# Both layers of the second MoE by one level of Strassen's scheme, with the sums of its weights' blocks parked in DRAM

## The chip, the cores and the metric

The kernel runs on one core of a Trainium2 chip. The metric is device time in microseconds (us) of one execution. Of the core's engines, TensorE (PE; its weight loads are listed as PEld) multiplies matrices, VectorE (DVE), ScalarE (ACT) and GpSimd (POOL) work on elements, and SyncE (SP) issues most DMAs.

## What is computed

Attention with a norm on q and k (4 batches, 12 heads, 448 positions, head size 64), then two MoE blocks one after the other on the 1792 x 768 result. The second is the one that changes:

```python
def _moe2_ref(x, w_in, w_out):      # x 1792x768, w_in 768x2048, w_out 2048x768
    h = x @ w_in
    relu6 = np.clip(h + 3.0, 0.0, 6.0)
    g = h * relu6 / 6.0
    return (g @ w_out).astype(np.float32)
```

Inputs and output are float32 on the host side, and the weights reach the chip as 64-bit floats, which the kernel decodes by integer operations on their two halves.

## The kernel before

Products that need float32's accuracy are made on float16: a matrix is scaled by a power of two and split into a high and a low part, and each product is three matmuls (high by high, low by high, high by low; `PROD`, L1208).

A planner (`Plan`) gets every step as an operation with its engine or engines, its dependencies, its buffer lease (`Ring`, `Lease`) and a modelled duration; it lists the steps by rank, shifted by offsets per stage (`CFG['off']`) and by a pace for the loads, and so writes one fixed order for each engine and for the DMA queue on SyncE. Where TensorE is expected to idle it adds filler matmuls on the identity (L1488).

The work goes by batch: attention, first MoE's input layer (L1218 in `in_block`, 448 columns), its output layer (L1271). Each batch's result (x2) is stored to DRAM. Attention of one batch is woven between the first MoE's matmuls of the one before. After the last batch the second MoE runs alone.

The second MoE goes over the tokens in five chunks (384 four times, then 256). Its input layer takes, for each of 16 blocks of 128 hidden features, 18 matmuls (6 blocks of 128 inputs by 3 parts) of the chunk's width into one PSUM bank (L1218); ScalarE's gate (L1364) reads the bank, VectorE multiplies (L1367), and the result is split into high (L410) and low (L425) in the tile gt. Its output layer takes, for each 128 tokens, 96 matmuls of 384 columns (L1385), copies the two banks out (L1404) and stores to the output (L1413).

The second MoE's weights W3 and W4 are prepared far ahead, within the batches from the first on (`Parked.add`, tile wc): 12 pieces of W3 are loaded as 128 x 1024 and 16 of W4 as 128 x 768 into two alternating buffers (wr), decoded by GpSimd (L525), VectorE (L532), ScalarE or GpSimd (L521, L516) and VectorE (L539), split with a common scale for each row, and stored as float16 parts (L649). When the first MoE's matmuls no longer need the SBUF places wa and wb, the parts are loaded back there (L681).

## Time and profile before

| what | us |
|---|---|
| median of 3 runs | 1240.18 (1237.2 to 1240.6) |
| span of the profiled execution | 1245.9 |
| TensorE busy | 1145.1 (92%) |
| VectorE busy | 757.2 (61%) |
| ScalarE busy | 705.1 (57%) |
| GpSimd busy | 393.6 (32%) |
| second MoE, first matmul to last | 801.4 to 1240.2 |

The profiled execution's span lies 5.7 us above the median of the runs. The profile is one execution; its views are the slices of the span, groups of instructions by source line and shape, busy time in windows, DMA issues, and the chain of work that ended last, followed back from the last instruction. A matmul's mean duration holds part of its neighbours', since matmuls overlap, so its share of time is the group's busy time over the count. TensorE's clock was at its upper level (2.4 GHz, granted share 1.00) in nearly all windows.

### The profile page before, as it was taken

Reading aid. Unit: us, or ns where it says so; the run is one execution under the profiler, and the core shown is the slowest. Engines: PE = TensorE matmul, PEld = TensorE weight load, DVE = VectorE, ACT = ScalarE, POOL = GpSimd, SP = SyncE. Lnnn points to the kernel's source line nnn. Section 1 sums busy time; section 2 is a strip of 40 time slices with the busy share of each in tenths; the row PEclk is TensorE's granted clock in tenths of the full one; section 3 lists DMA queues with packets and bytes.
Section 4 is the critical chain, followed back from the end, with each engine's and each line's share of the span. In section 5 each row is a group of like instructions: output and inputs, shape, how many; then the busy total and the mean of one; then the engine's idle time right before and its main releaser. Section 6 shows DMA issues by size and latency. Waiting matters only on the chain.

```text
span 1245.9 us, 19206 instructions
## 1 busy us (share of the span) xinstructions
PE 1145.1 (92%) x7151; PEld 654.0 (52%) x7151; DVE 757.2 (61%) x1326; ACT 705.1 (57%) x1512; POOL 393.6 (32%) x340
## 2 busy tenths in 40 slices
PE   2888898889797999989998899999999999999998
PEld 0555544444353455435454455566666666666684
DVE  7998799989889977699768775451041041041040
ACT  3888767888857787557778665541141141141140
POOL 6656667674747323456311221200000000000000
PEclk9999799999999999989999999999999999999999
DMA  6775567799986799866799876470100100100101
GB/s 177 209 192 175 175 193 205 170 193 221 224 261 185 186 193 229 262 188 191 155 193 247 240 252 225 137 215 14 47 18 13 46 19 14 40 12 13 26 1 26
DMA packets 253182, 180.05 MB, mean 145 GB/s; under 512 B 195488, under 2 KB 240544, under 8 KB 250016
## 3 DMA queue, kind: packets, MB, share of 16 engines
q1 hardware_dynamic: 251904, 177.66, 54.7%
q10 hardware_dynamic: 1184, 1.16, 0.4%
q8 instruction: 56, 0.92, 0.3%
q14 instruction: 38, 0.31, 0.1%
HBM read 96.01 MB, written 37.36 MB: 107 GB/s over the span
## 4 chain that ended last, share of the span: by engine, by line
PE 56%; DVE 8%; DMA 4%; issue 3%; ACT 2%; POOL 2%; SPq 1%; ACTq 0%; DVEq 0%; POOLq 0%
PE mm L1218 23%; PE s L1385 18%; PE mm L1271 10%; DMA arena<-phl 2%; PE mm L972 2%; DVE phl L425 1%; PE s L1011 1%; PE s L1014 1%; DVE smalls L782 1%; DMA arena<-in_q_dram 1%; POOL phl L440 1%; DVE arena L836 1%; DVE gt L425 1%; DVE st L1252 1%; ACT p L1024 1%
## 5 line engine op out<-in xcount | busy, mean ns | idle before, releaser
L1218 PEld LDWEIGHTS <-wa 128*128 128x128 f16 x2592 | 255.4, 99 | 193.4 <-issue 15.7
L1271 PE MATMUL mm<-gt,wb 128*128 128x448 f16 x1152 | 231.8, 356 | 10.1 <-POOL wb L440 4.0
L1218 PE MATMUL mm<-xt,wa 128*128 128x448 f16 x1152 | 231.0, 359 | 8.3 <-DVE st L1252 5.4
L1218 PE MATMUL mm<-arena,wa 128*128 128x384 f16 (+1 forms) x1440 | 219.6, 315 | 0.0
L1385 PE MATMUL s<-wb,gt 128*128 128x384 f16 x1344 | 219.2, 326 | 0.0
L1367 DVE SCALAR_TENSOR_TENSOR st<-st,mm 128x384 f32<-128x384 f32 (+1 forms) x80 | 42.1, 527 | 250.3 <-ACT st L1364 250.3
L1385 PEld LDWEIGHTS <-gt 128*128 128x128 f16 x1344 | 131.5, 98 | 86.8
L1271 PEld LDWEIGHTS <-wb 128*128 128x128 f16 x1152 | 112.6, 99 | 119.2 <-issue 6.1
L425 DVE SCALAR_TENSOR_TENSOR gt<-st,smalls,gt 128x448 f16<-128x448 f32 (+2 forms) x144 | 102.5, 717 | 51.7 <-ACT gt L410 50.5
L1024 ACT ACTIVATE p<-s,smalls 128x448 f32<-128x448 f32 x168 | 120.9, 721 | 17.6 <-DVE phl L425 6.6
L1404 ACT ACTIVATE p<-s,smalls 128x384 f32<-128x384 f32 x28 | 14.7, 577 | 199.6 <-PE s L1385 126.8
L410 ACT ACTIVATE gt<-st,smalls 128x384 f16<-128x384 f32 (+2 forms) x132 | 81.5, 621 | 78.3 <-DVE st L1367 46.0
L1019 DVE TENSOR_REDUCE smalls<-s 128x2 f32<-128x896 f32 (+1 forms) x96 | 92.0, 964 | 20.2 <-PE s L1014 19.7
L416 POOL TENSOR_SCALAR arena<-p,smalls 128x384 f16<-128x384 f32 (+1 forms) x13 | 9.9, 761 | 280.5 <-DMA p<-x2d 192.1
L1011 PE MATMUL s<-qkt 128*128 128x448 f16 (+1 forms) x192 | 62.9, 371 | 34.5 <-ACT p L1024 27.5
L1364 ACT ACTIVATE st<-mm,smalls 128x384 f32<-128x384 f32 (+1 forms) x80 | 51.7, 648 | 65.8 <-PE mm L1218 62.9
L425 DVE SCALAR_TENSOR_TENSOR phl<-p,smalls,phl 128x448 f16<-128x448 f32 x90 | 76.4, 875 | 9.6 <-ACT phl L410 5.7
L525 POOL TENSOR_SCALAR wc<-wr 128x1024 f32<-128x1024 f32 (+1 forms) x40 | 45.1, 1128 | 103.2 <-DMA wr<-in_moe_w_out_dram 75.2
L532 DVE SCALAR_TENSOR_TENSOR wc<-wr,wc 128x1024 uint32<-128x1024 uint32 (+1 forms) x40 | 46.9, 1171 | 31.7 <-POOL wc L525 31.7
L1014 PE MATMUL s<-qkt 128*128 128x448 f16 (+1 forms) x192 | 62.4, 366 | 0.0
L440 POOL TENSOR_TENSOR phl<-p,phl 128x448 f16<-128x448 f32 x31 | 43.4, 1409 | 49.4 <-ACT phl L410 43.4
L1073 PE MATMUL mm<-vhl,p 128*128 128x128 f32 x336 | 48.2, 299 | 9.5 <-ACT arena L1083 4.0
(165 smaller groups left out, 1566.1 us busy)
## 6 DMA issues: line engine op xcount, KB each, us to landing
wr<-in_moe_w_in_dram SPq DMA_DIRECT2D x16, 768.0 KB, 4.9
wr<-in_moe_w_out_dram SPq DMA_DIRECT2D x12, 1024.0 KB, 6.2
wr<-in_moe_w_in_dram SPq DMA_DIRECT2D x12, 1024.0 KB, 6.7
wr<-in_moe_w_out_dram SPq DMA_DIRECT2D x16, 768.0 KB, 4.7
qkd<-arena SPq DMA_DIRECT2D x18, 672.0 KB, 3.9
park_in<-wr SPq DMA_DIRECT2D x12, 512.0 KB, 4.4
park_out<-wr SPq DMA_DIRECT2D x16, 384.0 KB, 3.3
wa<-park_in SPq DMA_DIRECT2D x4, 1536.0 KB, 8.9
```

The costliest lines, as they stand in the source:

```text
L410: nc.scalar.activation(out=dst(), in_=src(), func=AF.Copy, scale=s)
L425: nc.vector.scalar_tensor_tensor(out=dst(), in0=src(), scalar=s, in1=high(), op0=ALU.mult, op1=ALU.subtract)
L440: (POOL, t_pool2(n), lambda: nc.gpsimd.tensor_tensor(out=lo(), in0=src(), in1=hi(), op=ALU.subtract)),
L1011: nc.tensor.matmul(o, lhsT=x[:, 64 * t:64 * t + m], rhs=x[:, 448:896], start=True, stop=False)
L1014: nc.tensor.matmul(o, lhsT=x[:, 64 * t:64 * t + m], rhs=x[:, 896:1344], start=False, stop=True)
L1019: nc.vector.tensor_reduce(out=nb, in_=s_t[sl.slot][:, :m, :S], axis=AX.X, op=ALU.max)
L1024: nc.scalar.activation(out=p(i), in_=s_t[sl.slot][:, i, :S], func=AF.Exp, bias=nb[:, i:i + 1], scale=alpha, accum_out=z[:, i:i + 1],)
L1073: nc.tensor.matmul(mm_t[tl.slot][:, 128 * j:128 * j + 128], lhsT=p(i)[:, c:c + 128], rhs=diag(), start=True, stop=True,)
L1218: nc.tensor.matmul(mm_t[ml.slot][:, :n], lhsT=w.inw(we, kc, f), rhs=x[:, xe, kc, :n], start=(kc == 0 and i == 0), stop=(kc == KD - 1 and i ...
L1271: nc.tensor.matmul(mm_t[ml.slot][:, :S], lhsT=W2.outw(we, fc, d * 128, 128), rhs=gv[:, ge_, fc, :], start=(fc == g.part.start and i == 0), ...
L1364: nc.scalar.activation(out=t, in_=m, func=AF.Relu, scale=ch.c3, bias=three)
L1385: nc.tensor.matmul(s_t[sl.slot][:, h, :half], lhsT=g[:, ge_, fc, tb * 128:tb * 128 + 128], rhs=W4.outw(we, fc, h * half, half), start=(fc ...
```

## The change

One level of Strassen's scheme (in Winograd's form) cuts each operand into 2 x 2 blocks, makes 7 products of sums of the blocks in place of 8 products of blocks, and gets the four blocks of the result by additions. Both layers of the second MoE are done so. The inner dimensions are halved: 768 into 2 x 384, the hidden 2048 first into two parts h (0 and 1), which are computed one after another, each of four `Quad`s (256 hidden features: two blocks of 128 by two halves of the chunk's tokens), and a `Pair` is 128 + 128 tokens by 2 x 384 outputs. There are three chunks of 768, 512 and 512 tokens. The turns are h = 0 for chunks 0, 1, 2, then h = 1 for chunks 2, 1, 0. The output sums of h = 0 are stored to a DRAM tile (part, L1785), loaded again with h = 1 (L1685) and added (L1735).

- A Quad has 7 products of 9 matmuls, each of half a chunk's columns (384 or 256), L1569; a Pair 7 of 12 with 384 columns, L1703. Bank 1 takes p1, p6, p5 and p3 on top of each other, and ScalarE copies it out between them (`keep`, L1589); the other results are additions on VectorE (L1582) into scratch, the gate (L1637) and product (L1640) run there, and seven sums (combine, L655) are split into high (L446, L452) and low (L669).
- The weights W3 and W4 come as 8 units each (128 x 1536 64-bit floats), one after another through one buffer: load L691, sign L703, decode L709, L719, L723, squares L739, four sums L655, high and low for 7 forms, store of 1344 KB L770. They begin after batch 1 (`wfrom`), not within batch 0, in the order W3 0 to 3, W4 0 to 3, W3 4 to 7, W4 4 to 7. The halves return by L778.
- x of a chunk is loaded (L1505, L1511), summed to 7 forms, split and stored once (L1529) for the second turn (L1537).
- Several tiles of SBUF are merged into larger ones, cut differently in different stages; the planner's numbers (`CFG`) are others. In the new order there are 131 filler matmuls instead of 202 (L1975).

```diff
-    CHUNKS = (384, 384, 384, 384, 256)
+    CHUNKS = (768, 512, 512)
+    FORMS = 7
+    HALF = 4
...
-    class Parked(Weight):
+    unit_ring, unit_loads, unit_stores = Ring(1), [], []
+    raw_u, set_u = cut(wr_m, 0, [128, 4 * LINE], I64), cut(wr_m, 12288, [128, 8, LINE], F32)
+    stage_u = cut(wr_m, 0, [128, 2, FORMS, LINE], F16)
...
+    class Combined:
...
+        def add(self, i, after):
+            n, here, unit = self.n, slice(i, i + 1), Lease(unit_ring)
...
+            o = sp(128 * n * (8 if self.wide else 4), load, after + unit_stores[-1:], takes=unit)
...
+            made = combine(self.left, lambda k: set_u[:, k], LINE, ends)
+            lows = []
+            for a, b in ((4, 7), (0, 4)):
+                flat = lambda t: t.rearrange("p a c -> p (a c)")
+                lows.append(parts(
...
+            self.stores[i] = sp(128 * 4 * FORMS * LINE, store, lows, gives=unit)
+            unit_stores.append(self.stores[i])
...
+    PAIRS = {1: (4, 4), 2: (5, 5), 3: (3, 6), 4: (6, 3), 5: (0, 0), 6: (1, 1), 7: (2, 2)}
+    BANK = {2: 0, 1: 1, 6: 1, 5: 1, 3: 1, 7: 2, 4: 2}
...
+    class Quad:
...
+            def emit():
+                for kc in range(3):
+                    for j, (we, xe) in enumerate(PROD):
+                        nc.tensor.matmul(
+                            self.bank(k), lhsT=w[:, we, fa, kc], rhs=self.ch.x[:, kc, xe, fb],
...
+        def keep(self, dst, deps, takes=None):
+            def emit():
+                nc.scalar.activation(out=self.held(dst), in_=self.bank(1), func=AF.Copy)
...
+        def p1(self):
+            self.product(1, [])
+            self.s1 = self.keep(0, [self.p[1]] + self.free, self.hold)
+        def p6(self):
+            self.product(6, [self.s1])
+            self.u2 = self.keep(1, [self.p[6], self.s1])
+        def p5(self):
+            self.product(5, [self.u2])
+            self.u4 = self.keep(2, [self.p[5], self.s1])
...
+        def p3(self):
+            self.product(3, [self.u4])
+            self.gate(7, 1, lambda: self.bank(1), [self.p[3]], self.banks[1])
...
+    def cycle(u, prev):
+        u.p1()
+        if prev is not None:
+            prev.p3()
+        u.p6()
+        if prev is not None:
+            prev.p4()
+        u.p5()
+        u.p7()
+        if isinstance(u, Pair):
+            u.p22()
+        u.p2()
...
-        if b == 0:
+        if b == CFG['wfrom']:
             off(7)
-            for i in range(W3.rows):
-                W3.add(i)
-            W3.add_scales(1.0)
+            for i in range(HALF):
+                W3.add(i, W2.done if i == 0 else [])
             off(8)
-            for i in range(W4.rows):
-                W4.add(i)
-            W4.add_scales(2.0 ** -21)
+            for i in range(HALF):
+                W4.add(i, [])
+            for i in range(HALF, 2 * HALF):
+                W3.add(i, [])
+            for i in range(HALF, 2 * HALF):
+                W4.add(i, [])
...
+    turns = [(0, ch) for ch in chunks] + [(1, ch) for ch in reversed(chunks)]
```

ScalarE in the second MoE. Before, in chunk 0 (st are float32 buffers, mm PSUM banks, gt the split result), gate and high part alternate:

```order
L1364 ACTIVATE st_72<-mm_92,smalls 128x384
L410 ACTIVATE gt<-st_72,smalls 128x384
L1364 ACTIVATE st_74<-mm_93,smalls 128x384
L410 ACTIVATE gt<-st_74,smalls 128x384
L1364 ACTIVATE st_73<-mm_90,smalls 128x384
```

Now, in a Quad of 256 columns (s_75 and s_76 are PSUM banks; p, st and wb hold scratch):

```order
L1589 ACTIVATE p<-s_75 128x256
L1637 ACTIVATE p<-st,smalls 128x768
L1589 ACTIVATE p<-s_75 128x256
L446 ACTIVATE gt<-p 128x768
L1589 ACTIVATE st<-s_76 128x256
L446 ACTIVATE gt<-p 128x1024
L1589 ACTIVATE st<-s_76 128x256
L1637 ACTIVATE wb<-s_75,smalls 128x256
```

The copies of bank 1 (L1589) now stand between gates and high parts of up to 1024 elements.

VectorE where the second MoE begins, before (product of the gate, low part):

```order
L1367 SCALAR_TENSOR_TENSOR st_72<-st_72,mm_92 128x384
L1367 SCALAR_TENSOR_TENSOR st_74<-st_74,mm_93 128x384
L405 TENSOR_SCALAR smalls<-smalls 128x1 x2
L425 SCALAR_TENSOR_TENSOR gt<-st_72,smalls,gt 128x384
L425 SCALAR_TENSOR_TENSOR gt<-st_74,smalls,gt 128x384
```

and now, in the first Quads of chunk 0:

```order
L1582 TENSOR_TENSOR p<-s_75,p 128x384
L1582 TENSOR_TENSOR p<-s_76,p 128x384
L709 SCALAR_TENSOR_TENSOR wr<-wr 128x768 x2
L1640 SCALAR_TENSOR_TENSOR wb<-wb,smalls,s_75 128x384
L723 SCALAR_TENSOR_TENSOR wr<-wr 128x768 x2
L1582 TENSOR_TENSOR p<-s_75,p 128x384
L655 TENSOR_TENSOR wr<-wr 128x384
```

Between the Quads' additions and gate products now stand decodes and sums of a unit of the weights (tile wr).

The DMA queue on SyncE near the end of the first MoE, before (park_out is W4's DRAM tile, x2d the first MoE's result):

```order
L649 DMA park_out<-wr_69 256x1x768
L1311 DMA x2d<-st_74 128x448
L509 DMA wr_69<-in_moe_w_out_dram 128x768
L1311 DMA x2d<-st_73 128x448
L649 DMA park_out<-wr_68 256x1x768
L649 DMA park_out<-wr_69 256x1x768
L681 DMA wb<-park_out 128x32x384 x2
```

and now:

```order
L770 DMA park_out<-wr 128x5376
L1529 DMA park_x_87<-xt 128x5376
L691 DMA wr<-in_moe_w_out_dram 128x1536
L1436 DMA x2d<-st 128x448
L778 DMA wb<-park_out 128x5376 x4
L770 DMA park_out<-wr 128x5376
L691 DMA wr<-in_moe_w_out_dram 128x1536
L770 DMA park_out<-wr 128x5376
```

Before, every piece of W4 was stored ahead of the reload into wb; now the last two units' stores stand behind it.

## Rows read from the trace of the kernel before

**Rows 1.** The page's slices of 31 us: busy tenths of two engines.
```profile
PE   2888898889797999989998899999999999999998
DVE  7998799989889977699768775451041041041040
```
**Rows 2.** The chain that ended last: start us, length us, what.
```profile
695.79 51.10 PE mm L1218 x270
746.89 54.48 PE mm L1271 x288
801.37 5.85 PE mm L1218 x36
...
1209.03 31.21 PE s L1385 x192
```
**Rows 3.** Groups of instructions by line and shape, TensorE: busy us, mean ns, idle before.
```profile
L1218 PE MATMUL mm<-arena,wa 128*128 128x384 f16 x1152 | 188.0, 326 | 0.0
L1218 PE MATMUL mm<-arena,wa 128*128 128x256 f16 x288 | 31.6, 273 | 0.0
L1385 PE MATMUL s<-wb,gt 128*128 128x384 f16 x1344 | 219.2, 326 | 0.0
L1218 PEld LDWEIGHTS <-wa 128*128 128x128 f16 x2592 | 255.4, 99 | 193.4 <-issue 15.7
L1488 PE MATMUL mm<-ident 128*128 128x512 bf16 x202 | 48.1, 388 | 1.2 <-DVE xt L1110 0.7 <-DVE smalls L390 0.5
```
**Rows 4.** Windows: us; busy us of PE, PEld, DVE, ACT, POOL; clock; DMA share; GB/s.
```profile
350.00:700.00 350.00, 322.42 (x2060) 167.90 (x2059) 287.08 (x504) 252.35 (x575) 139.93 (x121) 0.97 0.87 212
...
350.00:375.00 25.00, 25.00 (x135) 13.06 (x134) 23.07 (x43) 16.10 (x29) 13.61 (x12) 1.00 0.97 300
375.00:400.00 25.00, 20.45 (x101) 9.86 (x99) 24.27 (x48) 17.47 (x38) 17.31 (x13) 0.93 0.59 165
400.00:425.00 25.00, 20.57 (x101) 9.95 (x100) 24.15 (x35) 19.28 (x43) 11.72 (x11) 0.93 0.67 183
...
750.00:775.00 25.00, 25.00 (x134) 12.95 (x133) 11.13 (x23) 13.62 (x23) 4.94 (x5) 1.00 0.69 230
```
**Rows 5.** Groups by line and shape: ScalarE's and VectorE's steps on matrices.
```profile
L1364 ACT ACTIVATE st<-mm,smalls 128x256 f32<-128x256 f32 x16 | 9.0, 564 | 7.1 <-PE mm L1218 7.1
L410 ACT ACTIVATE wr<-wc,smalls 128x768 f16<-128x768 f32 x11 | 10.3, 933 | 4.1 <-DVE smalls L399 3.7
L410 ACT ACTIVATE wr<-wc,smalls 128x1024 f16<-128x1024 f32 x2 | 2.3, 1149 | 1.1 <-DVE smalls L399 1.1
L1367 DVE SCALAR_TENSOR_TENSOR st<-st,mm 128x256 f32<-128x256 f32 x16 | 6.7, 421 | 54.1 <-ACT st L1364 54.1
L425 DVE SCALAR_TENSOR_TENSOR gt<-st,smalls,gt 128x256 f16<-128x256 f32 x16 | 7.7, 484 | 9.2 <-ACT gt L410 9.2
L425 DVE SCALAR_TENSOR_TENSOR gt<-st,smalls,gt 128x384 f16<-128x384 f32 x64 | 39.7, 622 | 38.9 <-ACT gt L410 38.9
```
**Rows 6.** Groups by line and shape: decoding, low parts; last, GpSimd's in 350 to 700.
```profile
L532 DVE SCALAR_TENSOR_TENSOR wc<-wr,wc 128x768 uint32<-128x768 uint32 x16 | 15.3, 956 | 25.5 <-POOL wc L525 25.5
L425 DVE SCALAR_TENSOR_TENSOR wr<-wc,smalls,wr 128x1024 f16<-128x1024 f32 x9 | 13.0, 1446 | 1.7 <-ACT wr L410 1.2 <-POOL wr L416 0.5
L836 POOL TENSOR_TENSOR arena<-arena,smalls 128x448 f32<-128x448 f32 x15 | 17.5, 1189 | 14.1 <-DVE smalls L826 10.9 <-DVE smalls L405 3.3
```
**Rows 7.** DMA issues: KB each, median us to landing.
```profile
wa<-park_in SPq DMA_DIRECT2D x4, 1536.0 KB, 8.9
```
**Rows 8.** Windows, only instructions on tile wc: busy us of DVE, ACT, POOL.
```profile
350.00:700.00 350.00, 54.22 (x44) 20.11 (x33) 31.86 (x23) 0.97 0.87 212
```
**Rows 9.** VectorE's groups in 375 to 400, 400 to 425, 750 to 775 us.
```profile
L425 DVE SCALAR_TENSOR_TENSOR gt<-st,smalls,gt 128x448 f16<-128x448 f32 x4 | 5.1, 1267 | 0.0
L425 DVE SCALAR_TENSOR_TENSOR gt<-st,smalls,gt 128x448 f16<-128x448 f32 x7 | 4.9, 738 | 0.0
L425 DVE SCALAR_TENSOR_TENSOR gt<-st,smalls,gt 128x448 f16<-128x448 f32 x1 | 0.7, 674 | 0.0
```

More of the change, by code (lines that the diff above doesn't have):

```diff
@@ L195, in order @@
             o.missing, o.ready = len(o.deps), [0.0] * 5
-            for l in o.also + [x for x in (o.takes, o.gives) if x is not None]:
+            for l in o.also + o.takes + ([] if o.gives is None else [o.gives]):
                 l.todo, l.free, l.slot = l.left, 0.0, None
@@ L232, in order @@
                 wait[w[0]].remove(o)
[L233 to L237 removed]
+            for l in o.takes:
+                l.slot = l.ring.when(l)[1]
+                l.ring.held[l.slot] = l
+                l.ring.given += 1
             o.way = way
@@ new lines, in join_scales, with largest, spread_out, scales @@
+    def join_scales(h):
+        part_ = slice(HALF * h, HALF * h + HALF)
+        both, most, big, fac = small(HALF), small(), small(), small(HALF)
+        k3, k6 = small(HALF), small(HALF)
+        lease = Lease(mm_ring)
+        e16 = most.bitcast(BF16)[:, :1]
+        line = lambda: mm_t[lease.slot][:, :128]
+        def largest():
+            nc.vector.tensor_tensor(out=both, in0=W3.e[:, part_], in1=W4.e[:, part_], op=ALU.mult)
+            nc.vector.tensor_reduce(out=e16, in_=both, axis=AX.X, op=ALU.max)
+        def spread_out():
+            nc.tensor.matmul(line(), lhsT=e16.to_broadcast([128, 128]), rhs=ident16, start=True, stop=True)
+        def scales():
+            nc.vector.tensor_reduce(out=big, in_=line(), axis=AX.X, op=ALU.max)
+            inverse(most, big, 0)
+            times(fac, both, most, 2.0 ** -16)
+            nc.vector.tensor_single_scalar(out=k3, in_=fac, scalar=3.0, op=ALU.mult)
+            nc.vector.tensor_single_scalar(out=k6, in_=fac, scalar=6.0, op=ALU.mult)
+        o = op((DVE, 300, largest), W3.scaled[part_] + W4.scaled[part_])
+        o = op((PE, 300, spread_out), [o], takes=lease)
+        o = op((DVE, 1000, scales), [o], gives=lease)
+        return o, big, fac, k3, k6
@@ new lines, in keep, with store, load, back @@
+        def keep(self):
+            for k in range(3):
+                def store(k=k):
+                    queue().dma_start(out=self.park[k], in_=self.x[:, k].rearrange("p e f c -> p (e f c)"))
+                self.kept[k] = sp(128 * 4 * FORMS * self.n, store, self.ready[k])
+        def load(self, after):
+            self.ready = []
+            for k in range(3):
+                def back(k=k):
+                    queue().dma_start(out=self.x[:, k].rearrange("p e f c -> p (e f c)"), in_=self.park[k])
+                l = sp(128 * 4 * FORMS * self.n, back, [self.kept[k]] + after)
+                self.ready.append([l, l])
@@ new lines, in attention_moe_moe_kernel @@
+    last_users = end.pvs + end.xlow
+    pairs_done = {}
+    W3.back_done, W4.back_done = [None, None], [None, None]
+    W3.back_done[0] = [W3.back(i, end.inlast[-1:]) for i in range(HALF)]
+    W4.back_done[0] = [W4.back(i, end.outlast[-1:]) for i in range(HALF)]
+    chunks, c0 = [], 0
+    for j, n in enumerate(CHUNKS):
+        chunks.append(Chunk(j, c0, n))
+        c0 += n
+    joined = [join_scales(0), join_scales(1)]
+    prev, wr_free = None, unit_stores[-1:]
+    chunks[0].prepare((2, 2, 2), {2: last_users}, end.inlast[-1:])
```

682 lines of the change are left out of this document (494 added, 188 removed).

## Prediction

> **What bounds the kernel now.** I read the page's slices first: TensorE's digits are 8 and 9 in the first two thirds and 9 to the end, while VectorE falls from 9 to between 0 and 5 for the last third [rows 1]. The chain that ended last says where: from 695.8 us to the end it runs on TensorE alone, 51.1 and 54.5 us of the first MoE's last batch, then from 801.4 us the second MoE, ending at 1240.2 us with 31.2 us of its output layer [rows 2]. So the second MoE is 439 us of back-to-back matmuls, and only fewer or shorter matmuls shorten it. Its groups of lines say of what: 1152 matmuls of 384 columns and 288 of 256 in the input layer, 1344 of 384 in the output layer, together 188.0 + 31.6 + 219.2 = 438.8 us [rows 3]; TensorE waits for nothing there. Ahead of it two things share the bound: between 350 and 700 us VectorE is busy 287.1 of 350 us, TensorE 322.4 [rows 4]. Stretches such as 375 to 400 and 400 to 425 us, with VectorE at 24.3 and 24.2 of 25 us and TensorE at 20.5 and 20.6, are bound by VectorE [rows 4].
>
> **TensorE's saving.** Strassen makes 7 products of 8. Of the input layer the columns become half a chunk: 8 Quads of 63 matmuls with 384 columns and 16 of 63 with 256; of the output layer 14 Pairs of 84 with 384. At the rows' 163.2, 109.7 and 163.1 ns each (busy time over count, 188.0/1152, 31.6/288, 219.2/1344, since matmuls overlap and the mean of one, 326, holds its neighbour's) that is 504 × 163.2 = 82.2, 1008 × 109.7 = 110.6 and 1176 × 163.1 = 191.8, in sum 384.6 us [rows 3]. The term is **-54.2 us**. A weight load takes 99 ns on its own part of the engine [rows 3], still under the 109.7 ns of the short matmul, so I cost it nothing; were the short ones to take 130 ns, it would be +20 us.
>
> **What the other engines do beside it.** Before, an accumulation went to one bank, and the gate read it. Now each Quad copies bank 1 out three times between its products (p1, p6, p5) and adds the copies to other banks. For a Quad of 256 columns, from the nearest rows [rows 5]: ScalarE high parts of 768 (0.93) and often 1024 (1.15), which is 0.84 ns an element and 0.29 us, by which 3 copies of 256 cost 0.50 each; gates of 256 (0.56) and 768 (about 0.99): 5.1 us. VectorE 3 additions of 0.42, gate products of 0.42 and 0.95, low parts of 768 and 1024 by the two forms of L425 (0.484 for 256, 0.622 for 384: 1.08 ns an element and 0.21 us) 1.04 and 1.31, about one form's sum of 0.6: 5.6 us. GpSimd 3 or so sums of forms (its row is 1189 ns for 448 columns, so 0.7 for 256, [rows 6]) and at times a high part of 1024: 3.2 to 4.7 us. TensorE's Quad is 63 × 0.1097 = 6.91 us. All three fit, with little to spare.
>
> **Stalls of the second MoE: +15 us** (6 to 40). (a) p6 writes on in bank 1 once the copy of p1 has left it. Between them stands one product of the previous Quad, 0.99 us; the copy takes 0.50, which leaves 0.49 us for two hand-overs between the engines; no row shows one alone, and I take it that they just fit. Whatever ScalarE does ahead of a copy is not covered: the order has a high part of 1024 elements (1.15 us) between two copies that p6 and p5 wait for. Four or five of the six turns have such a pair of places at about 1 us: 5 us. (b) At a turn's change the first Quad's gate writes a scratch which the last Pair's store (786 KB) still reads; by the row of 1536 KB in 8.9 us [rows 7] that store is 4.6 us, of which the other products cover all but about 1 us; five changes: 5 us. (c) The start: two units of the weights are still to be decoded when the Quads begin (order of VectorE and SP), in the memory that chunk 1's x also needs, and the first weights, 4 × 1344 KB for each layer, come back in the same 55 us as x0's parts and two units. That is some 19 MB, of which the best stretch that moves data, 300 GB/s between 350 and 375 us [rows 4], brings 16.5 in 55 us. What is late by that, 8 us, mostly falls on the units and not on the first Quad: 5 us, between 0 and 25.
>
> **The front: +11 us** (-5 to +31). Each of the 16 units costs VectorE, by the 768-element form, 4 decodes of 956 ns (3.8), low parts of 2688 elements at 1446/1024 ns (3.8), and about a third of its 4 sums (1.0 us each for 384 columns, scaled from GpSimd's 1189 ns for 448; 1.3): 8.9 us [rows 6]. Ten of them lie before 700 us: 89 us, where the old pieces took 54.2 us of VectorE [rows 8]. That is 35 us more; between the rows of ordinary work that the order keeps in both, from batch 1's gates to batch 2's, I count 25 us. ScalarE gets 22 us more and GpSimd 40, and both have the room (GpSimd is busy 139.9 of 350 us [rows 4]). The decoding used to start inside batch 0 and now starts after batch 1, so what it leaves free earlier is not taken by anything that the chain shows. VectorE is above 93% in five stretches of 25 us out of fourteen (the first two of them in [rows 4]), 36%; 36% of some 31 us is 11. Against it: the order has 131 filler matmuls instead of 202, and 71 × 238 ns (48.1/202) = 17 us are TensorE idle time that the planner counts on no more [rows 3]; hence -5 as the lower end. Upper end: all 31.
> Sum: -54.2 + 15 + 11 = -28.2 us. The profiled execution is 1245.9 us, 5.7 above the median of the runs; the difference is carried over to the median: 1240.2 - 28.2 = **1212.0 us**.
>
> **Rivals.**
> A. No stalls to speak of, front unchanged: stalls 6, front -2: 1240.2 - 50 = 1190. For it: TensorE has no idle row in 439 us and the other engines fit on average. Against: three copies per Quad have next to no cover.
> B. VectorE bounds the Quads. The same low part of 448 columns takes 674 ns in 750 to 775 us, where GpSimd does 4.9 of 25 us, 738 in 400 to 425 with 11.7, and 1267 in 375 to 400 with 17.3 [rows 4, 9]. A Quad has GpSimd at 3.2 to 4.7 of 6.91 us (46 to 68%), between the last two rows, and 3.9 of VectorE's 5.6 us has two operands in the same memory. At ×1.10 a Quad's VectorE work is 6.0 us and hidden; at ×1.5 it is 7.55, so 0.64 late in each of 16, and about 0.4 in each of the 8 wide ones (10.28 us of TensorE): +14, 1226.
> The Trainium skill, "SBUF — State Buffer", "Who interferes with whom", says that a VectorE instruction with two inputs in SBUF contends with a GpSimd instruction that reads SBUF, and that the later of the two waits out the whole of the other. The rows agree in kind; were all of GpSimd's 4.7 us to fall on VectorE, a Quad would take 10.3 us, and 16 × 3.4 = 54 us would cancel the change; no run here shows that much.
> C. Slower than before: the single buffer of the units. Each unit's load waits for the unit before to be stored, where before two buffers alternated. From rows the steps of one add to 8.9 us (load, 1536 KB, [rows 7]) + about 14 (sign, decodes, square, parts, by the forms in [rows 5, 6]) + 8 (1344 KB) = 31 us. The first load goes at about 352 us; the last store must be out by about 874, before chunk 1's x is needed (801 + 11 + 82 of chunk 0's first turn, less 20 to prepare x): 522/16 = 32.6 us for each. Every further us costs up to 16, and from 34.4 us a unit (16 × 1.8 = 28 us more) the kernel is slower than before; 35 us gives 1212 + 16 × 2.4 = 1250. Against it: the order puts u10's load near 688 us, 34 us a unit in the busy stretch with much slack in between, and later units have little else on VectorE (11.1 busy of 25 us in 750 to 775 [rows 4]).
> D. The short matmuls run at 130 instead of 110 ns: +20, 1232. The 288 such matmuls of the old kernel ran at 109.7 ns [rows 3].
>
> **How the numbers follow.** Forecast 0.50, A 0.20, B 0.13, C 0.12, D 0.05. About 0.3% (3.7 us) is what a measurement of this kernel can tell from no change. Faster by more than that, under 1236.5: A, the forecast but for its upper tail, D and most of B: 0.81. Within: 0.07, from the ends of B and the forecast. Slower: C, 0.12. The range of 8 in 10 leaves out C and a little of A's lower part: 1187 (A with a shorter front) to 1238 (B and D with large stalls).
>
> **What would show it.** The second MoE's start at 812 us instead of 801, and its length 439 - 54 + 15 = 400 us; a matmul line of the Quads at 163 and 110 ns; TensorE's idle time there put down to ScalarE's copies (a), to a store (b), and to a load at the start (c). B: VectorE above 95% in the Quads and low parts over 1.9 us for 1024 elements. C: the last two units' loads after 860 us, and TensorE waiting for chunk 1's x. I am wrong about the front if VectorE's load in 350 to 700 us grows and the first MoE's end stays at 801 us.

## The result and the profile after

The changed kernel takes 1255.14 us, the median of 4 runs (1253.34 to 1257.86); the kernel before 1239.45 beside it (1237.2 to 1240.6). The ratio is 1.0122, with a 95% interval of 1.0098 to 1.0147: 1.2% slower, where 1212.0 was forecast, outside the range of 1187 to 1238. The profiled execution has a span of 1251.8 us.

The page's slices of the changed kernel, 31 us each, answer to [rows 1]:

```profile
PE   3788869787887889984999899998898999999988
DVE  7998999978799977799977677568747454545472
```

TensorE's last third no longer is a row of nines, and VectorE's last fourteen digits, 0 to 5 before, are 2 to 8. The chain that ended last does not run on TensorE alone in the second MoE any more, as it did in [rows 2]. Of the matmuls it shows (start us, length us, what; L1569 is a Quad's product, L1703 a Pair's):

```profile
842.97 1.46 PE s L1569 x9
...
905.10 1.95 PE mm L1703 x12
...
986.04 2.95 PE mm L1569 x27
```

Nine of 384 columns take 1.46 us (162 ns each), twelve of a Pair 1.95 (163 ns), 27 of 256 columns 2.95 (109 ns): the steps of [rows 3] hold. The time lies between them. Windows cut at the changed kernel's batches 1, 2, 3 and its second MoE (us; busy us of PE, PEld, DVE, ACT, POOL; clock, DMA share, GB/s):

```profile
343.00:513.00 170.00, 147.38 (x916) 75.34 (x914) 147.72 (x225) 128.56 (x276) 90.57 (x76) 0.95 0.83 207
513.00:682.00 169.00, 146.81 (x921) 75.46 (x920) 138.93 (x241) 121.49 (x257) 58.81 (x53) 0.93 0.84 218
682.00:821.00 139.00, 134.56 (x764) 70.38 (x763) 97.66 (x137) 69.61 (x111) 53.37 (x41) 0.99 0.62 210
821.00:1247.00 426.00, 395.71 (x2693) 264.70 (x2690) 243.44 (x343) 163.52 (x269) 153.33 (x139) 0.98 0.36 132
```

The same three batches of the kernel before, from the run before_again below:

```profile
353.00:505.00 152.00, 142.65 (x904) 73.53 (x903) 131.51 (x218) 116.48 (x270) 69.08 (x58) 0.98 0.89 213
505.00:668.00 163.00, 152.68 (x957) 78.81 (x956) 130.56 (x226) 113.42 (x257) 66.92 (x58) 0.97 0.81 203
668.00:799.00 131.00, 124.03 (x714) 65.54 (x713) 82.74 (x166) 80.28 (x142) 28.74 (x27) 0.99 0.73 227
```

The second MoE starts at 821.0 us, where it started at 801.4 in [rows 2] and 799.1 in before_again, and takes 426.0 us instead of 439.0. Matmuls of 384.6 us were to be done in it, so 41.4 us are lost there: for 30.3 of them TensorE stands idle, and it is busy 11.1 us longer than reckoned, at a granted clock of 0.98 where the kernel before had 1.00. So 13 of the 54 us saved are left, and ahead of the second MoE 20 us are given up. That is a balance of two: batch 0, in which the second MoE's weights are no longer prepared, ends 10 us earlier (at 343 us, before at 353), and the batches 1 to 3 together take 478 us instead of 446, 32 more. In these batches neither kernel has the clock at its upper level throughout (0.93 to 0.99 in the rows above; of the 32 windows of 25 us ahead of 800 us in the first profile of the kernel before, 13 are below 1.00). What stands ahead of the prediction, the upper level in nearly all windows, holds for the second MoE alone.

By the medians the loss ahead of the second MoE is larger. An execution of the kernel before ends 446.5 us behind the start of its second MoE (1245.59 against 799.1 in before_again), so a median one of 1240.2 starts it at about 793.7; the execution of [rows 2] was a longer one. The changed kernel's profiled execution took 1253.6 us, 432.6 from that start, so its median one of 1255.1 starts it at 822.5. Reckoned so, the front, which is all that lies ahead of the second MoE, lost some 29 us.

### The profile page after: what moved, and what is told of

Read it like the earlier page. It is cut to its first block, busy times and chain, and to the rows that moved or that the text cites. A ratio compares the mean times of both kernels' runs of the same rounds, so it can differ in the third digit from the quotient of the medians.

```text
span 1251.8 us, 19224 instructions
## 1 busy us (share of the span) xinstructions
PE 1091.4 (87%) x7000; PEld 639.3 (51%) x7000; DVE 925.7 (74%) x1464; ACT 743.5 (59%) x1539; POOL 595.6 (48%) x513
## 4 chain that ended last, share of the span: by engine, by line
PE 31%; DVE 14%; ACT 6%; DMA 5%; POOL 3%; issue 3%; SPq 0%; ACTq 0%; POOLq 0%; DVEq 0%
PE s L1703 7%; PE mm L1396 7%; PE mm L1703 5%; PE mm L1343 5%; DVE gt L669 3%; PE mm L1569 3%; PE s L1569 3%; DMA xt<-p 3%; POOL p L655 2%; DVE p L1640 1%; DVE p L461 1%; POOL wa L655 1%; DVE wr L669 1%; PE mm L1097 1%; ACT wb L1637 1%
## 5 line engine op out<-in xcount | busy, mean ns | idle before, releaser
L1569 PEld LDWEIGHTS <-wa 128*128 128x128 f16 x1512 | 147.9, 98 | 63.5 <-issue 18.0
L1703 PEld LDWEIGHTS <-gt 128*128 128x128 f16 x1176 | 116.7, 99 | 97.0 <-issue 18.4
L1569 PE MATMUL s<-xt,wa 128*128 128x256 f16 (+1 forms) x882 | 123.6, 291 | 14.0 <-ACT st L1589 7.6
L1703 PE MATMUL s<-wb,gt 128*128 128x384 f16 x672 | 122.1, 330 | 15.5 <-ACT wb L1727 9.3
L655 POOL TENSOR_TENSOR wr<-wr 128x384 f32<-128x384 f32 (+1 forms) x60 | 66.1, 1108 | 75.6 <-DVE wr L723 38.1
L1136 PE MATMUL s<-gt 128*128 128x448 f16 (+1 forms) x192 | 63.9, 380 | 37.4 <-ACT p L1149 31.7
L1703 PE MATMUL mm<-wb,gt 128*128 128x384 f16 x504 | 95.5, 336 | 0.7 <-ACT wa L1727 0.7
L703 POOL TENSOR_SCALAR wr<-wr 128x768 f32<-128x768 f32 x32 | 38.1, 1189 | 113.4 <-DMA wr<-in_moe_w_in_dram 56.1
L461 DVE SCALAR_TENSOR_TENSOR p<-p,smalls 128x448 f16<-128x448 f32 x90 | 79.5, 909 | 12.1 <-ACT p L446 11.4
L1569 PE MATMUL mm<-xt,wa 128*128 128x256 f16 (+1 forms) x630 | 85.9, 289 | 0.0
L655 POOL TENSOR_TENSOR p<-p 128x256 f32<-128x256 f32 (+1 forms) x50 | 60.1, 1209 | 50.0 <-DVE p L1640 41.5
L446 ACT ACTIVATE p<-p,smalls 128x448 f16<-128x448 f32 (+1 forms) x100 | 63.1, 658 | 24.4 <-DMA xt<-p 17.1
L655 POOL TENSOR_TENSOR wa<-wb 128x256 f32<-128x256 f32 (+1 forms) x14 | 15.1, 1085 | 126.5 <-DVE wb L1640 126.5
L1139 PE MATMUL s<-gt 128*128 128x448 f16 (+1 forms) x192 | 63.3, 374 | 0.0
L461 DVE SCALAR_TENSOR_TENSOR gt<-st,smalls,gt 128x448 f16<-128x448 f32 x64 | 54.9, 877 | 6.0 <-ACT gt L446 5.3
```

The lines of the kernel that those rows point to most:

```text
L446: nc.scalar.activation(out=dst(), in_=src(), func=AF.Copy, scale=s)
L461: nc.vector.scalar_tensor_tensor(out=dst(), in0=src(), scalar=s, in1=high(), op0=ALU.mult, op1=ALU.subtract)
L655: eng.tensor_tensor(out=f(o), in0=f(a), in1=f(b), op=how)
L1136: nc.tensor.matmul(o, lhsT=x[:, 64 * t:64 * t + m], rhs=x[:, 448:896], start=True, stop=False)
L1139: nc.tensor.matmul(o, lhsT=x[:, 64 * t:64 * t + m], rhs=x[:, 896:1344], start=False, stop=True)
L1569: nc.tensor.matmul(self.bank(k), lhsT=w[:, we, fa, kc], rhs=self.ch.x[:, kc, xe, fb], start=first and kc == 0 and j == 0, stop=kc == 2 and ...
```

## The experiments

All leave the order of instructions as the change has it, unless said otherwise: a step left out leaves a hole in the order and moves nothing. The changed kernel and the four edits that leave its front whole (no_sums, sums_unread, sums_dve, short_copies) start the second MoE between 820.3 and 823.8 us, so a shift of the start by 3 or 4 us shows nothing by itself.

**before_again.** No edit.

> The kernel before once more, unchanged, for its profile. The first profile's span (1245.9 us) is longer than every listed run (1237.2 to 1240.6). Theory: that execution lost 7 to 8 us ahead of the second MoE, which runs on TensorE alone for 439 us and has nothing to lose; then here the second MoE starts at 793 to 795 us, not 801, and the changed kernel's 821 is 26 to 28 us late instead of 20. Rival: the span of a profiled execution is always that much longer than the timed ones; then it starts at about 801 again.

1241.94 us (1237.91 to 1248.23), start at 799.1 us in an execution of 1245.59. The executions of the kernel before differ by 10 us. The second MoE took 439.0 us in both profiles, with TensorE never idle, so I take the 10 us to lie ahead of it; no short execution was profiled.

**two_units_less.** Of the last two units of W4 only the squares' sum and the scale are left; the loads, the other steps and the stores (L770) are empty.

```diff
+            if not self.left and i >= 2 * HALF - 2:
+                for o in plan.ops[k0:]:
+                    if o is not q and o is not q0:
+                        o.ways = [(w[0], w[1], lambda: None) for w in o.ways]
```

> The changed kernel in its order, without the work of the last two units of W4 (their load, decoding, sums, parts and store; only the sum of squares and the scale stay, and the two units before them are loaded in their place, so the output is another one). Theory: in the first turn of the second MoE, which takes 97 us for 82 us of matmuls, about 7 of the 15 us are VectorE's and GpSimd's work on these units: the turn takes 88 to 91 us and the whole 1246 to 1249. Rival, the wide Quads bind VectorE by themselves: the turn stays at 95 or more, the whole at 1252 or more.

1244.74 us, second MoE 411.4 us. Windows cut at the turns of the changed kernel (first, second, third and last of six), and then the first two turns of this one:

```profile
821.05:918.15 97.10, 84.84 (x484) 48.31 (x483) 67.96 (x86) 45.49 (x63) 45.48 (x36) 0.95 0.51 196
918.15:979.05 60.90, 57.15 (x421) 41.69 (x421) 39.60 (x67) 25.78 (x45) 25.48 (x25) 0.97 0.22 77
979.05:1037.45 58.40, 55.78 (x422) 41.07 (x421) 28.96 (x46) 21.24 (x40) 15.20 (x16) 1.00 0.37 138
...
1154.55:1247.07 92.52, 86.62 (x530) 51.54 (x527) 45.69 (x55) 29.06 (x43) 27.60 (x21) 1.00 0.14 40
```

```profile
826.30:908.80 82.50, 79.41 (x485) 47.22 (x484) 48.56 (x71) 38.25 (x56) 28.47 (x26) 1.00 0.41 159
908.80:968.00 59.20, 55.44 (x421) 41.03 (x421) 40.34 (x67) 25.95 (x45) 25.55 (x25) 1.00 0.23 79
```

The first turn falls from 97.1 to 82.5 us, the 82.2 of its matmuls; VectorE from 68.0 to 48.6 us, GpSimd from 45.5 to 28.5. The other turns stay within 2 us. So the last two units cost 14.6 us, twice what I expected here. Of these, 9.2 are idle time of TensorE and 5.4 its busy time: the same matmuls took 84.8 us at a granted clock of 0.95, and 79.4 at 1.00. So here the loss was larger than TensorE's wait. (The whole gained 10.4: the start came 4 to 5 us later, in the median too, which stays unexplained.)

**no_sums, sums_unread, sums_dve.** The four sums after each gate are left out; are made but not read; are made by VectorE.

```diff
-                eng.tensor_tensor(out=f(o), in0=f(a), in1=f(b), op=how)
+                if not skip:
+                    eng.tensor_tensor(out=f(o), in0=f(a), in1=f(b), op=how)
...
-                    lambda a=a, b=b: f(a, b), 1.0, (b - a) * self.n,
+                    lambda a=a, b=b: f(a + 4 * (a < 4), b + 4 * (a < 4)), 1.0, (b - a) * self.n,
...
-                [(POOL, t_pool2(n), lambda emit=emit: emit(nc.gpsimd)), (DVE, t_dve_two(n) / 1.6, lambda emit=emit: emit(nc.vector))],
+                [(POOL, t_pool2(n), lambda emit=emit: emit(nc.vector if dve else nc.gpsimd)), (DVE, t_dve_two(n) / 1.6, lambda emit=emit: emit(nc.vector))],
```

> The changed kernel in its order, without the 4 sums of forms after each of the 24 gates of the second MoE (GpSimd mostly, some on VectorE), so that the split takes old values and the output is another one. Theory, the sums are slower than planned beside VectorE (1.0 to 1.9 us each where I had 0.7 to 1.0) and stand in the chain from a turn's last gate to the Pairs: the second MoE takes 405 to 412 us instead of 426, the whole 1236 to 1242. Rival, the copies of bank 1 and the front's units are the loss: the second MoE stays at 420 or more.

> The changed kernel in its order; the 4 sums of forms after each gate are made as before, but the split reads the gated blocks in their place, so that nothing waits for the sums (the output is another one). Leaving the sums out took the second MoE from 426 to 399 us. Theory, what costs is the waiting for slow sums in the chain from a turn's last gate to the Pairs: the second MoE takes 402 to 408 us here too. Rival, it is their claim on memory beside VectorE's two-operand instructions: it takes 417 or more, and the low parts of 1024 stay near 1485 ns (1243 without the sums).

> The changed kernel in its order, with the sums of the second MoE's gates that GpSimd makes (1.0 to 1.9 us each) made by VectorE at the same place of the order; the output is the reference's. Theory, GpSimd's sums are slow and slow VectorE's two-operand instructions at the same time, while VectorE without them is busy 204 of 399 us: a sum of 256 takes 0.5 us on VectorE, the chain at a turn's end has two changes of engine less, and the second MoE takes 404 to 412 us, the whole 1233 to 1241. Rival, VectorE then binds the Quads: 420 us or more.

1228.66, 1246.09 and 1245.29 us; the second MoE takes 399.0, 415.7 and 415.7 us. Without the sums the turns (first, second and last) are:

```profile
823.80:912.00 88.20, 81.48 (x485) 47.40 (x484) 60.16 (x84) 45.27 (x63) 23.91 (x22) 0.98 0.56 216
912.00:967.50 55.50, 55.08 (x420) 41.06 (x420) 34.24 (x63) 25.81 (x45) 10.49 (x12) 1.00 0.24 84
...
1136.10:1222.80 86.70, 86.26 (x529) 51.53 (x527) 37.11 (x52) 28.40 (x43) 8.43 (x8) 1.00 0.15 42
```

Turns of 512 tokens come to 55.5 to 56.4 us, near the matmuls' 55.0, and the last to 86.7, 4.5 above its matmuls'. So the sums cost 27 us. They do not add to the 14.6 of the two units: 8.9 of the 27 lie in the first turn, whose whole loss of 14.9 goes with the units' work as well. In the other turns the sums cost 18.1 us, and 8.4 are lost there without them; with the 14.9 these are the 41.4. Both theories hold a part: if nothing waits for the sums, 10 us come back, and the rest only when they are gone. In sums_unread the low parts stay as slow as in the changed kernel (644 ns for 256, 1484 for 1024), so these 10 us are the waiting alone. Why the sums cost more than their time, VectorE's and GpSimd's groups in the second MoE show; changed kernel, then no_sums, then sums_dve (busy us, mean ns, idle before):

```profile
L669 DVE SCALAR_TENSOR_TENSOR gt<-p,gt 128x256 f16<-128x256 f32 x28 | 17.7, 644 | 2.7 <-ACT gt L446 1.9 <-POOL gt L452 0.9
L669 DVE SCALAR_TENSOR_TENSOR gt<-wa,gt 128x1024 f16<-128x1024 f32 x8 | 11.9, 1485 | 3.7 <-POOL gt L452 2.5 <-ACT gt L446 1.2
L655 POOL TENSOR_TENSOR p<-p 128x256 f32<-128x256 f32 x28 | 28.4, 1024 | 26.9 <-DVE p L1640 26.2
```

```profile
L670 DVE SCALAR_TENSOR_TENSOR gt<-p,gt 128x256 f16<-128x256 f32 x28 | 11.4, 432 | 1.7 <-ACT gt L446 1.4
...
L670 DVE SCALAR_TENSOR_TENSOR gt<-wa,gt 128x1024 f16<-128x1024 f32 x8 | 9.9, 1243 | 0.5 <-ACT gt L446 0.5
```

```profile
L669 DVE SCALAR_TENSOR_TENSOR gt<-p,gt 128x256 f16<-128x256 f32 x28 | 13.2, 486 | 1.3 <-POOL gt L452 1.2
...
L655 DVE TENSOR_TENSOR p<-p 128x256 f32<-128x256 f32 x32 | 12.9, 414 | 0.1
```

The low part of 256 takes 644 ns beside GpSimd's sums, 432 without, 486 with the sums on VectorE; that of 1024 takes 1485 and 1243. A sum of 256 takes 1024 ns on GpSimd, 414 on VectorE. And where the sums stand in the way, the changed kernel's chain of waits shows, in the Quads of the fifth turn:

```profile
1118.61 1.03 DVE p L1640
...
1119.71 0.74 POOL p L655
...
1120.52 0.80 POOL p L655
...
1121.39 1.33 POOL p L655
...
1122.74 1.06 ACT gt L446
...
1123.83 1.22 DVE gt L669
...
1128.98 1.03 PE s L1569 x8
```

From the gate's product (L1640) over three sums on GpSimd (L655) to high (L446) and low part (L669) it is a string of steps on VectorE, GpSimd, ScalarE and VectorE, one behind the other; in this chain TensorE comes next at 1128.98 us, behind more steps of VectorE and ScalarE.

**short_copies.**

```diff
-                nc.scalar.activation(out=self.held(dst), in_=self.bank(1), func=AF.Copy)
+                nc.scalar.activation(out=self.held(dst)[:, :8], in_=self.bank(1)[:, :8], func=AF.Copy)
```

> The changed kernel in its order; the copies of bank 1 between a Quad's products take 8 of its 256 or 384 columns (the output is another one), so a copy costs ScalarE little more than its start, 0.25 us less. Theory (a) of the prediction, the copies have no cover: TensorE waits for them 8.8 us in the trace, and the second MoE takes 420 to 423 us instead of 426. Rival, what is late there is what stands ahead of the copies on ScalarE and VectorE: it takes 425 or more.

1258.7 us, second MoE 428.9: nothing gained. TensorE's waits in the second MoE of the changed kernel (who waited for whom, us, times, longest):

```profile
PE s L1703 <- ACT wb L1727: 9.3, 5, 3.9
PE s L1569 <- ACT st L1589: 7.6, 8, 1.7
PE s L1703 <- DVE gt L669: 4.3, 3, 2.4
...
PE s L1569 <- ACT p L1589: 1.2, 2, 0.7
```

The same copies of the Quads (L1589) and Pairs (L1727) in no_sums, where these lines are L1590 and L1728:

```profile
PE s L1704 <- ACT wb L1728: 1.2, 5, 0.2
...
PE s L1570 <- ACT st L1590: 1.0, 2, 0.5
```

TensorE waits 7.6 us for the Quads' copies, and shorter copies leave 6.6 of it. Without the sums 1.0 is left, and 1.1 where the sums are made but not read: what is late is what ScalarE does ahead of a copy, and that waits for the sums. The Pairs' copies, 9.3 us, are late until the sums are gone (1.2; 10.2 in sums_unread). A wait names the last link, not the cause.

**no_lows** and **no_unit_sums.** The units' low parts are left out; the units' sums are left out.

```diff
         def low():
+            if skip:
+                return
...
-            made = combine(self.left, lambda k: set_u[:, k], LINE, ends)
+            made = combine(self.left, lambda k: set_u[:, k], LINE, ends, skip=True)
```

> The changed kernel, its order of instructions as it is, with the 32 low parts of the units (VectorE, 3.8 us a unit) left out; the store takes the high parts twice, so the output is another one. Theory, VectorE's work for the units sets the time ahead of the second MoE: 14 units x 3.8 = 53 us of VectorE less before it, of which 40 to 60% is on the path, 20 to 30 us; the second MoE starts at 791 to 801 us instead of 821, the whole takes 1225 to 1235 us. Rival, the new planner's numbers and the order made the front slow, or the single buffer: the start moves by less than 6 us and the whole stays above 1247.

> The changed kernel in its order, without the 4 sums of each unit (38 on GpSimd at 1.2 us and 18 on VectorE at 0.87 us ahead of the second MoE); the split takes the plain blocks in their place, so the output is another one. VectorE's low parts of the units take 1963 ns for 1536 elements and 865 ns for the attention's 448 (751 when the units were left out). Theory, GpSimd's sums slow VectorE's two-operand steps by some 25 us in all, and with their own 16 us are the larger part: the second MoE begins at 805 to 813 us. Rival, the wait for the sign is: it begins at 816 or later. In the first turn of the second MoE, where the last two units stand, 97 us should become 90 to 94 either way.

1241.56 and 1242.41 us; starts at 816.5 and 809.5 us; first turns 88.3 and 94.8 us. Taking 49 us of VectorE's steps out of the front gives 4.5 us, hardly more than one execution differs from the next; taking out the sums gives 11.5.

**no_units, order_alone, transfers_only.** The units' work and their transfers: work left out, with the stores' source a small block of zeros read over and over; also no loads and only two stores; and the full loads and stores with no work but one write of zeros by GpSimd.

```diff
+            for k, o in enumerate(plan.ops[k0:], k0):
+                if o is not unit_loads[-1] and o is not self.stores[i] and not k1 - 1 <= k < k2:
+                    o.ways = [(w[0], w[1], lambda: None) for w in o.ways]
```

> The changed kernel in its order, with nothing left of the 16 units but their loads, stores (of zeros, so the output is another one), scales and a short sum of squares: no decoding, no sums, no parts. Without the low parts alone the second MoE began at 816.5 us against 821.0. Theory, the units' work on VectorE, GpSimd and ScalarE together (9 us of VectorE, 6 of GpSimd, 5 of ScalarE a unit) sets the time ahead of the second MoE: it begins at 790 to 800 us, and the whole takes 1200 to 1212 us. Rival, the order that the planner's new numbers write, with attention's steps ahead of the gates on VectorE, is slow by itself: it begins at 810 or later, the whole takes 1222 or more.

> The changed kernel in its order, with nothing left of the units but scales, a short sum of squares and the store of the first unit of each layer (zeros, so the output is another one); no loads and no other stores, whose small pieces took 11 us each when all units stored zeros. Theory, the order written around the units sets the time ahead of the second MoE, whatever runs in their places: it begins at 812 to 825 us, as with the units (821). Rival, their transfers on the DMA queue are what the attention's loads wait for: it begins at 805 or earlier.

> The changed kernel in its order, with the 16 units' loads and stores at their full length and nothing else of them but scales, a short sum of squares and one GpSimd write of zeros for each (so the output is another one). With the units the second MoE begins at 821.0 us, without their work and transfers at 804.1, without their low parts at 816.5. Theory, the engines' work (sign, decoding, sums, parts) is the 17 us: it begins at 803 to 808 us here. Rival, the 46 MB of loads and stores on the one DMA queue hold up the attention's own transfers: it begins at 815 or later.

1247.62, 1223.05 and 1218.43 us; starts at 829.4, 804.1 and 801.0; the second MoE takes 411 to 413 us in all three. The first is a miss of mine: the stores of zeros changed the transfers as well as the work. The other two show what the engines' work on the units costs in this order: without it, with all transfers, the second MoE starts 20 us earlier and its first turn takes 81.8 us instead of 97.1; with the work it is 36.7 us of the median more. The batches 1, 2, 3 of transfers_only:

```profile
345.00:507.00 162.00, 145.69 (x926) 75.54 (x925) 102.39 (x189) 106.73 (x262) 58.08 (x54) 0.97 0.94 222
507.00:668.00 161.00, 146.97 (x933) 76.00 (x932) 102.64 (x214) 105.04 (x250) 42.22 (x35) 0.96 0.91 233
668.00:801.00 133.00, 128.70 (x747) 67.80 (x746) 49.10 (x97) 44.59 (x88) 26.76 (x19) 1.00 0.67 225
```

They take 456 us, against 478 with the work. Of the 22, some 15 are idle time of TensorE, and 7.4 its busy time (428.8 and 421.4 us for 2601 and 2606 matmuls), again at a lower clock. The wait of the first MoE's matmuls for VectorE's product of the gate, in the changed kernel, transfers_only and before_again:

```profile
PE mm L1343 <- DVE st L1377: 17.0, 4, 12.9
```

```profile
PE mm L1354 <- DVE st L1388: 10.6, 3, 8.3
```

```profile
PE mm L1218 <- DVE st L1252: 4.4, 1, 4.4
```

What the two runs do not settle is the comparison with the kernel before. Its batches take 446 us with the work on its own pieces of W3 and W4 in them, and no run left that work out. So an order without any such work that needs 456 us may well cost something of its own, against which the earlier end of batch 0 stands; how the 20 us divide between more work and an order that hides it less stays open.

**sign_on_act** and **later_units_sign.** The sign step by ScalarE. A copy times zero turned out not to keep the sign: the outputs of these two kernels, later_units_sign below being the other, are those of weights that are all positive. The steps and their shapes are the same, so their times stand.

```diff
-                    nc.gpsimd.tensor_scalar(
-                        out=c[:, cut_], in0=high(F32), scalar1=2.0 ** -126, scalar2=2.0 ** -126, op0=ALU.mult, op1=ALU.mult
-                    )
+                    nc.scalar.activation(out=c[:, cut_], in_=high(F32), func=AF.Copy, scale=0.0)
```

> The changed kernel in its order; the sign step that opens a unit's decoding (32 times 768 elements, 1.2 us each on GpSimd) is made by ScalarE at the same place (a copy times zero keeps the sign, about 0.92 us). Ahead of the second MoE VectorE stands 29.9 us in wait for that step, with the attention's and the gates' steps queued behind. Theory, this waiting in line is the larger part of the units' 20 us: the second MoE begins at 806 to 814 us instead of 821. Rival, the units cost by their own time on VectorE (120 us of 478): it begins at 817 or later.

1254.8 us, start at 820.7. VectorE's wait only has another name now (us, times, longest):

```profile
DVE wr L707 <- ACT wr L703: 28.4, 10, 15.2
```

In the changed kernel it was 29.9 us for GpSimd's L703. So in this order it is not GpSimd's making of the sign that costs. What VectorE's waiting itself costs, my theory, this run leaves open, since the wait stayed nearly as long.

**all_sums_dve.** sums_dve, with the units' sums on VectorE too.

> The changed kernel in its order, with the sums of the units and of the gates that GpSimd makes (60 and 72 of them, about) made by VectorE at the same place; the output is the reference's. Leaving out the units' sums moved the start of the second MoE from 821.0 to 809.5 us, making the gates' sums on VectorE its length from 426 to 416. Theory, it is GpSimd's 1.2 us and its claim on memory that cost, not the sums as such: 0.55 us each on VectorE, start at 812 to 816 us, length 412 to 415, the whole 1236 to 1242. Rival, VectorE has no room for them ahead of the second MoE: start at 821 or later.

1245.61 us, start at 825.1, second MoE 413.7: the rival. Sums that cost 11.5 us of the front where GpSimd makes most of them cost it no less where VectorE makes them all; I take it that VectorE has no room for them there.

```profile
L655 DVE TENSOR_TENSOR wr<-wr 128x384 f32<-128x384 f32 x56 | 34.5, 638 | 0.1
```

**old_numbers1.** The planner's numbers of the kernel before in the changed one, so another order.

> The changed kernel with the planner's numbers of the kernel before (offsets, paces, biases of the engines, look-ahead), and the units begun after batch 1 as in the change; the output is the reference's. Theory, the new numbers are what makes the front slow: the second MoE begins at 800 to 812 us instead of 821. Rival, the units need the new numbers: it begins at 822 or later.

1318.43 us, start at 838.0, and a first turn of 140.8 us; the last unit's store leaves at 948.3 us, in the changed kernel at 883.9. The new numbers are not the cause, they are a remedy.

**later_units, later_units_sums.** A version with another order: three units of W4 taken up behind the x of chunks 1 and 2, the scales of h = 1 joined only when its first turn comes, offsets and paces searched anew, the gates' sums by VectorE, and in the second of the two the units' sums as well.

```diff
-            for i in range(HALF, 2 * HALF):
+            for i in range(HALF, 2 * HALF - 3):
                 W4.add(i, [])
...
+                for i in {0: [5], 1: [6, 7]}.get(turn, []):
+                    W4.add(i, sum(nxt.ready, []))
+                    wr_free = unit_stores[-1:] + wr_free
```

> A version of the changed kernel; the output is the reference's. Unit 5 of W4 is taken up behind chunk 1's x, units 6 and 7 behind chunk 2's x, so that 13 units instead of 16 lie ahead of turn 1; the gates' sums are made by VectorE; the planner has other offsets and paces. Theory, the number of units that the order has to fit ahead of the second MoE sets its start, and the last ones slow its first turn: it begins at 790 to 800 us (821), takes 405 to 415 us (426), the whole 1205 to 1222, faster than both kernels. Rival, the late units only move their cost into turns 1 and 2: the second MoE takes 425 or more.

> The version with three units of W4 taken up in turns 1 and 2, the gates' sums on VectorE and other planner's numbers (1237.6 us), with the sign step of the units on ScalarE as well; the output is the reference's. If the wait for the sign is the larger part, the second MoE begins at 797 to 801 us instead of 806.7 and the whole takes 1226 to 1233 us; if it is not, 1234 to 1240.

> The version with three units of W4 in turns 1 and 2, the gates' sums on VectorE and other planner's numbers (1237.6 us), with the units' sums on VectorE as well; the output is the reference's. Theory as for the run before: the second MoE begins at 799 to 803 us instead of 806.7 and takes 420 to 424 us instead of 425, the whole 1228 to 1234, faster than both kernels. Rival: 1236 or more.

1237.61, 1224.87 and 1229.43 us. later_units starts the second MoE at 806.7 us, and its second MoE takes 425.0: there the rival was right, the third turn went from 58.4 to 64.9 us with two units in it. later_units_sums starts its second MoE at 796.1 us and takes 426.2 for it; against the kernel before it is 0.9914 (0.9886 to 0.9942), faster than both kernels. Unlike in all_sums_dve, the sums on VectorE gain here, by 8 us; that this is because three units fewer lie ahead is my reading, since order and numbers differ too. later_units_sign gains 12.7 us on later_units (start 801.0, second MoE 419.8), by an edit that gave nothing in the changed kernel; that stays unexplained.

## Why the prediction was wrong

**TensorE's saving: right.** 109 and 163 ns a matmul, and without the sums the turns of 512 tokens come down to their matmuls but for 0.5 to 1.4 us. D falls.

**"All three fit, with little to spare": the step that failed first.** My mean of an engine's work in a Quad said nothing of the Quad whose results are needed next: the last one of a turn runs gate, sums, high and low part one behind the other, and the Pairs wait for the end of it. The sums were in the list of GpSimd's work, at 0.7 us, and in none of the stalls (a) to (c): as a stall they were put at nothing. They cost 27 us, and the stalls, forecast at 15, came to 41.4. Of B's mechanism, which had a chance of 0.13 and a price of 14, the rows bear out a part: the low parts are lengthened by 49% (256) and 19% (1024), where B needed 50% on all. The Trainium skill, "SBUF — State Buffer", "Who interferes with whom", has a VectorE instruction with two inputs in SBUF contend with a GpSimd instruction that reads SBUF. The runs agree on who is slowed: the average low part of 256 takes 212 ns more beside sums of 1024 ns, and a sum of 256 on VectorE (into wa) 842 ns in the changed kernel, 417 in sums_dve. These are averages over steps that met one of GpSimd and steps that met none, so they do not show what a single meeting costs.

**Stalls (a), (b), (c).** (a), 5 us: right as far as it went. The copies just fit, as I took it, and what stands ahead of them on ScalarE makes TensorE wait, 7.6 us in the trace; but that work is late because of the sums, which (a) did not see. (What I called theory (a) at short_copies, the copies' own length, was not what (a) had priced.) (b), 5 us: the turn changes show one wait, of 1.3 us, and not for a store. (c), 5 us "between 0 and 25": the right place and the wrong mechanism; 14.6. I had priced the lateness of a transfer. With all transfers and none of the units' work the first turn has its 81.8 us, so it is the work: I had hidden the two units' 18 us of VectorE (19.4 measured) in a turn that seemed to have room beside the Quads' own 49. Why it has none, bursts of the Quads or GpSimd beside them, no run tells apart.

**The front: +11, measured +20 in the profiled pair, some +29 by the medians.** The price of a unit on VectorE was right, 8.9 us: the rows of the changed kernel between 343 and 821 us add to 28.3 + 27.6 + 27.5 + 21.4 + 15.6 = 120.4 us for 14 units, 8.6 each.

```profile
L461 DVE SCALAR_TENSOR_TENSOR p<-p,smalls 128x448 f16<-128x448 f32 x78 | 65.2, 865 | 9.5 <-ACT p L446 8.7 <-POOL p L452 0.5
...
L709 DVE SCALAR_TENSOR_TENSOR wr<-wr 128x768 uint32<-128x768 uint32 x28 | 28.3, 1023 | 29.9 <-POOL wr L703 29.9
L723 DVE SCALAR_TENSOR_TENSOR wr<-wr 128x768 int32<-128x768 int32 x28 | 27.6, 1012 | 1.8 <-ACT wr L719 1.7
L669 DVE SCALAR_TENSOR_TENSOR wr<-wr,smalls 128x1536 f16<-128x1536 f32 x14 | 27.5, 1963 | 1.3 <-ACT wr L446 0.9 <-POOL wr L452 0.4
...
L669 DVE SCALAR_TENSOR_TENSOR wr<-wr,smalls 128x1152 f16<-128x1152 f32 x14 | 21.4, 1532 | 1.4 <-ACT wr L446 1.3
...
L655 DVE TENSOR_TENSOR wr<-wr 128x384 f32<-128x384 f32 x18 | 15.6, 871 | 0.1
```

What failed is the step from there to the path: "36% of some 31 us", a share of stretches as a factor. The batches 1 to 3 lost 32 us; and batch 0, whose earlier end I had put at nothing, gave 10 back. In the changed order the units' work alone is 20 us on the path. The units also lengthen what others do; the attention's low part (L461) is 865 ns above and 751 where only the transfers run:

```profile
L461 DVE SCALAR_TENSOR_TENSOR p<-p,smalls 128x448 f16<-128x448 f32 x78 | 56.2, 751 | 44.2 <-ACT p L446 35.3 <-POOL p L452 8.7
```

And VectorE's time was a poor measure: its low parts, 40% of a unit's, gave 4.5 us, the sums, mostly on GpSimd, 11.5. How these two and the decoding share the rest is open: leaving out one step shifts what the next waits for, and no run left out the decoding alone.

**The base.** I carried over the profile's 5.7 us as if they lay anywhere. As far as the two profiles show, they lay in the front of the kernel before, so the profiled pair shows 7 us of loss where the medians show 15.7. With stalls of 41 and a front of 29 in place of 15 and 11, the sum comes to +16.

**The rivals.** C, the chance of 0.12 for slower, named the chain of single units and its end at 874 us; the last store left at 883.9 us. But its price was to be paid by chunk 1's x, and TensorE did not wait for that: its one wait where chunk 1 begins, 1.3 us, is for a Pair's addition on VectorE. Nor were the last two units' loads behind 860 us (822.9 and 850.8). The units cost by the work they put beside the Quads and the gates. So slower came true by other mechanisms than the one that I had given for it; that C's chance of 0.12 met the outcome was luck.

## What to carry to other kernels

Where a trick takes matmuls away and adds sums and splits, look at the last block before a dependent layer and add up its steps over all engines in a row; engine averages hide it. Work that is hidden in a stretch before has room only until the engine there is full: cost it by leaving it out of the changed order (steps emptied, order kept), which told work from transfers in two runs, and leave the old work out of the old order too, which was not done here. And move helper sums off GpSimd only where VectorE has the time: the same edit gave 10 us in one stage and none in another.

## What was not expected of the hardware

The stores of zeros in no_units, whose source was read in pieces of 128 bytes, took 11.1 us for 1344 KB, where the changed kernel's take 5.6 (KB each, median us to landing):

```profile
park_in<-zero SPq DMA_DIRECT2D x8, 1344.0 KB, 11.1
```

```profile
park_in<-wr SPq DMA_DIRECT2D x8, 1344.0 KB, 5.6
```

With 16 of them the second MoE began at 829.4 us, later than with all the units' work (821.0) and 28 us later than with the full transfers (801.0): here a transfer's form cost more than all the engines' work on the units did (20 us). And one sum of two float32 blocks of 256 columns takes GpSimd 0.73 to 1.32 us in the changed kernel, by its place in the string, and VectorE 0.84 there but 0.41 to 0.42 in sums_dve, where GpSimd makes none of a gate's sums.
